# A kernel of attention and a gated feed-forward net: three passes in place of five from a maximum to a power of two and its inverse, and a new order of the whole program

## The chip, the cores and the metric

The kernel runs on one core of a Trainium2 chip. The metric is the device time of one execution in microseconds (us). The engines are TensorE (PE, matmuls), VectorE (DVE), ScalarE (ACT), GpSimd (POOL) and SyncE (SP), which only starts transfers. Each takes its instructions strictly in the order in which the program holds them, and waits by semaphores for what others produce.

## The reference

```python
def _attn_ref(q, k, v) -> np.ndarray:
    ...
    q_d = q.reshape(B, H, Sd, factor, D).mean(axis=3)
    ...
    out_d = sm_attn(q_d, k_d, v_d)
    out_up = np.repeat(out_d, factor, axis=2)
    pos = np.arange(S)
    mask = np.abs(pos[:, None] - pos[None, :]) < factor
    scores = scale * np.matmul(q, k.transpose(0, 1, 3, 2))
    scores = np.where(mask, scores, -1000000000.0)
    ...
    return (out_up + out_local).astype(np.float32)
...
def _moe_ref(x, w_in, w_spatial, b_spatial, w_out) -> np.ndarray:
    h = np.maximum(x @ w_in, 0.0)
    ...
    u, v = (h[..., :d_ff // 2], h[..., d_ff // 2:])
    ...
    v_n = (v - mu) / np.sqrt(var + 1e-06)
    v_s = np.einsum('ts,bsd->btd', w_spatial, v_n) + b_spatial[None, :, None]
    gated = u * v_s
    return (gated @ w_out).astype(np.float32)
```

q, k and v have 8 batches of 8 heads with 576 rows of 64 elements, and factor is 4; w_in is 512 x 1024, w_spatial 576 x 576, w_out 512 x 512. Attention over groups of four rows and local attention in a band of seven are added; the sum x goes through a feed-forward net with a gate along the sequence.

## The kernel before

**Numbers.** The large products are done in f16, with both factors split into a high and a low half, and three of the four partial products taken. For a factor to be split, it is first scaled by a power of two that follows from a bound on its sizes. Such a bound is made in `bound`: ScalarE sums sizes by row, TensorE turns the column of sums (L479), DVE takes the greatest (L482) and keeps its exponent (L483), TensorE spreads it over the 128 partitions into PSUM (L486), and DVE makes the power of two and its inverse from it in `exponents` (L499 to L503): a copy out of PSUM, an AND that keeps the exponent's bits, a multiply by −1 with a limit, and two passes that add constants. Eleven calls do so: the V half and the U half of w_in, w_out, and the eight batches of x. The bound of w_spatial (`columns`) takes the same function without a value from PSUM. The gate uses `bound` with passes of its own (L1105 to L1107).

**Work.** Each batch is four pieces of two heads. A piece takes sums of four rows (L720, L723), scores in the band (S, L748) with the mask either laid down by two matmuls on TensorE (L741) or added by DVE (L761), their maximum and difference (L770, L776; L764, L767 with the mask on DVE), exponentials on ScalarE (L788, L791), inverse of the row sums (L797, L801), norms (L836), the same for the down-sampled attention (Sd L810, L852 to L876), transposes (T L844, Td L891), products with v (AV L952, AVd L919), the sum xf of both (L971, L973), and the high half (xhi, L1002, ScalarE) and the low half (xlo, L1004, DVE) of x. The tiles xa to xf are x of a piece, sxa and sxb the scales of a batch, sw the scales of the weights. Then comes the net, batch by batch: V (L1029), U (L1092), the gate's product with w_spatial (SP, L1124 to L1127) with the gating on DVE (L1145, L1135), and O (L1160), twelve matmuls of 512 columns a group. The weights are decoded (L542, L547) and split into a high half on ScalarE (L510) and a low half on DVE (L513; L573 and L587 for the short last rows of w_spatial and the bias). `warm` (L1204) puts filler matmuls into TensorE's list.

**Order.** Nothing is emitted in the order of the code. Every step is an operation with an engine, a cost in ns, what it reads and writes, and a rank; `run` keeps a clock by these costs and emits for each engine the operation of least rank among those that can start within NEAR of the first. The ranks are the piece or batch number plus offsets from tables (RANK, MRANK, WRANK), less EVICT for work that empties PSUM; STAY favours the kind of matmul that TensorE is at (large f16, or the small f32 ones of the attention). Where a step can be done by one of several engines, a letter for each piece in ON says which (D DVE, P GpSimd, A ScalarE; for the mask, T TensorE and D DVE; the last letter holds for all further pieces).

```python
t, _, ask, o = min((x for x in found if x[0] <= first + near), key=lambda x: (x[1], x[0]))
...
bound(lambda: sx.ap, NP, parts, sx.sub(8), rank, powers(lambda: sx.ap, 1.0, 0.0, 30.0), 740)
...
pe_mask = sc.pick == "T"
```

Of the kernel before, what the change touches and what calls it, by code (L numbers as in the profile page):

```python
# [252 lines left out]
RANK = {"load": [143.005, 47.751, 252.982, -69.47, -172.22, -274.786, 560.411, -758.364, -311.459, 313.434, 266.06, 380.575,  # L253
            943.336, 399.915],
        "vload": [391.404, 86.345, 272.249, 337.531, 429.684, -52.69, -370.895, -252.053],
        "vabs": [509.637, -1181.093, -217.316, 87.185, -457.776, 123.004, -794.489, 144.366],
        "tv": [-183.93, 240.18, 765.617, 930.011, 56.071, -19.127, -157.242, 125.859],
        "sum": [-115.268, 142.997, -94.455, -372.167, 362.55, -75.596, 306.456, 702.576, 1696.966, 425.169, -234.075, 705.288,
            -421.357, 223.437],
        "S": [-1061.927, -157.575, 379.809, -830.223, -915.099, 670.631, 141.564, -649.896, 467.386, 88.454, 513.148, 238.256,  # L260
            245.41, 202.772],
        "E": [-534.894, -339.729, -702.236, 21.188, 160.003, 471.872, 219.972, 899.326, -409.142, -823.461, -265.585, -479.069,
            -503.017, -440.633],
        "N": [231.109, -483.572, -754.504, 524.152, -141.085, 397.308, 1325.226, -80.846, -320.013, -220.077, -64.133, -498.673,
            700.859, -253.394],
        "T": [-347.227, -440.539, -1149.413, -139.403, 917.828, -1374.545, -1166.794, 234.909, 536.972, -105.532, -561.257,
            -49.343, -383.904, -24.157],
        "Sd": [-228.884, 341.247, -989.571, 12.731, -290.563, 65.584, -210.501, 584.996, 760.783, -156.288, -493.755, 182.161,
            -206.462, -81.893],
        "Nd": [20.186, -634.328, -625.655, -47.029, -1024.698, 6.919, -369.885, -166.975, -196.395, -51.441, 745.233, 26.68,  # L270
            590.548, 680.939],
        "Td": [226.557, -226.969, 765.057, -163.935, 412.294, -360.224, 842.794, -998.859, 11.321, 28.445, -152.942, 58.045,
            -1153.807, -259.463],
        "AVd": [377.528, -777.682, -319.581, 176.718, 599.105, 1049.442, -339.489, -191.118, -286.676, -150.229, -415.778,
            -182.501, -118.84, 141.634],
        "AV": [60.151, -170.544, -717.724, 720.142, -836.725, 275.504, 440.562, -339.226, -949.724, 57.757, -184.347, -239.42,
            -4.966, -560.047],
        "X": [49.462, -601.369, 382.04, -619.469, -420.239, 803.995, 16.415, -27.426, 201.671, 266.124, -288.114, 118.52,
            -424.608, -87.751]}
MRANK = {"V": [[-120.813, 103.137], [-373.166, -785.223], [-588.287, 86.439], [-457.053, -295.554], [-271.069, 53.075],  # L280
            [-161.929, 7.172], [-384.75, 67.584], [1.753, -86.54]],
        "U0": [[-381.018, 507.475], [-225.844, -398.15], [392.079, 353.99], [415.277, -261.891], [-69.09, -16.703], [-362.251,
# [23 lines left out]
        "WO load": [201.774, -325.888, 429.457, 987.307],  # L306
        "WO decode": [137.835, 619.019, -225.889, -8.083],
        "WO bound": [-64.148, 457.463, -289.1, 18.247, -58.582],
        "WO split": [620.04, -563.746, 894.059, 1022.164]}
# [940 lines left out]
```

## Time and profile before

| | |
|---|---|
| median of three runs | 579.53 us (578.91 to 579.99) |
| profiled execution | 580.97 us, of it span 579.1 |
| PE busy | 551.6 us (95%), 6501 matmuls |
| DVE busy | 414.1 us (72%), 1084 instructions |
| ACT busy | 376.3 us (65%), 1076 instructions |
| POOL busy | 186.7 us (32%), 213 instructions |
| granted TensorE clock | 0.995 of full speed over the span |

The profile shows one execution, so its times are held against 580.97 us and not against the median. The busy shares are means over a start in which weights and the first batch are prepared (to 72.4 us), batch 0 of the net up to its first output (to 117.4 us), and the long rest, in which TensorE does the net of a batch and, between, the attention of later pieces.

### The profile page before, as it was taken

What the parts mean: (1) busy time and instruction counts of PE and PEld (TensorE: products, weight loads), DVE (VectorE), ACT (ScalarE), POOL (GpSimd) and SP (SyncE); (2) the same over time, 40 slices, a digit from 0 to 9 for tenths busy, and PEclk for the clock granted to TensorE, in tenths of its full rate; (3) what the DMA queues carried; (4) which work ended last, traced back from release to release, by engine and by line L of the source; (5) the groups of instructions that cost most, each with busy time, mean ns of one, the idle gap of its engine ahead of it and who ended that gap; (6) DMA issues with size and microseconds to landing.
All of it is one profiled execution on the core that took longest, in us unless ns stands there. A gap on an engine that the chain in (4) does not pass through costs nothing.

```text
span 579.1 us, 16048 instructions
## 1 busy us (share of the span) xinstructions
PE 551.6 (95%) x6501; PEld 368.0 (64%) x6501; DVE 414.1 (72%) x1084; ACT 376.3 (65%) x1076; POOL 186.7 (32%) x213
## 2 busy tenths in 40 slices
PE   5877899999999998999999999999999999999996
PEld 2445547764786566765776747778567567756752
DVE  5989899964898888578687776781976666844420
ACT  3689999457577677567575877565756665954422
POOL 3636533023531254154330432422422352202100
PEclk9999999999999999999999999999999999999999
DMA  8987870035322344225303343214220400010012
GB/s 285 338 241 213 215 180 1 1 102 143 88 83 91 115 103 126 65 90 138 86 20 119 99 113 102 84 65 108 77 100 2 138 2 19 8 32 1 20 54 74
DMA packets 37390, 57.04 MB, mean 99 GB/s; under 512 B 3650, under 2 KB 24130, under 8 KB 37316
## 3 DMA queue, kind: packets, MB, share of 16 engines
q1 hardware_dynamic: 35012, 48.94, 26.7%
q0 software_dynamic: 2304, 7.08, 7.2%
q8 instruction: 51, 0.84, 0.6%
q14 instruction: 23, 0.19, 0.1%
HBM read 46.57 MB, written 9.44 MB: 97 GB/s over the span
## 4 chain that ended last, share of the span: by engine, by line
PE 70%; DVE 18%; ACT 6%; issue 2%; DMA 2%; POOL 0%; SPq 0%; ACTq 0%; DVEq 0%; POOLq 0%
PE pmd L1124 4%; PE pma L1124 4%; PE pmb L1160 4%; PE pma L1160 4%; PE pmc L1029 4%; PE pmc L1160 4%; PE pma L1029 4%; PE pmc L1124 3%; PE pmb L1124 3%; PE pmd L1029 3%; PE pmd L1092 2%; PE pma L1092 2%; PE pmc L1092 2%; PE pmb L1029 2%; PE pmd L1160 2%
## 5 line engine op out<-in xcount | busy, mean ns | idle before, releaser
L1092 PEld LDWEIGHTS <-win 128*128 128x128 f16 x768 | 74.7, 98 | 20.8 <-issue 0.6
L1124 PEld LDWEIGHTS <-vha 128*128 128x128 f16 x768 | 74.0, 98 | 20.6 <-issue 2.1
L1160 PEld LDWEIGHTS <-gb 128*128 128x128 f16 x264 | 25.6, 98 | 28.5 <-issue 0.4
L1124 PE MATMUL pma<-wsp,vha 128*128 128x256 f16 (+1 forms) x216 | 29.4, 286 | 0.0
L1124 PE MATMUL pmd<-wsp,vha 128*128 128x256 f16 (+1 forms) x204 | 27.6, 285 | 1.3 <-DVE aua L1105 1.3
L1204 PE MATMUL pma<-mask_b,mask_a 128*128 128x512 bf16 x83 | 23.4, 415 | 3.1 <-DVE mask_a L383 3.1
L1124 PE MATMUL pmb<-wsp,vha 128*128 128x256 f16 (+1 forms) x180 | 24.1, 283 | 0.0
L1124 PE MATMUL pmc<-wsp,vha 128*128 128x320 f16 (+1 forms) x168 | 23.5, 290 | 0.0
L1160 PE MATMUL pmb<-wo,gb 128*128 128x512 f16 x96 | 22.0, 379 | 0.0
L1160 PEld LDWEIGHTS <-ga 128*128 128x128 f16 x120 | 11.6, 98 | 12.8 <-issue 0.2
L1057 POOL TENSOR_TENSOR sta<-sta,mhalf 128x1 f32<-128x1 f32 (+1 forms) x14 | 9.0, 646 | 32.3 <-DVE sta L1041 32.3
L669 POOL DMA_DIRECT2D tvb<-v_dram x12 | 10.8, 900 | 18.2 <-DMA tvb<-v_dram 15.7
L1160 PE MATMUL pma<-wo,gb 128*128 128x512 f16 x72 | 16.5, 379 | 0.0
L1029 PEld LDWEIGHTS <-xa 128*128 128x128 f16 x96 | 9.2, 98 | 10.8 <-issue 0.2
L1204 PEld LDWEIGHTS <-mask_a 128*128 128x128 bf16 x85 | 7.9, 104 | 12.6 <-issue 3.7
L720 POOL TENSOR_TENSOR suma<-qka 128x576 f32<-128x576 f32 x6 | 7.8, 1294 | 23.4 <-DMA qka<-qk_dram 23.4
L669 POOL DMA_DIRECT2D tva<-v_dram x12 | 10.8, 902 | 13.2 <-DMA tva<-v_dram 8.9
L1057 POOL TENSOR_TENSOR stb<-stb,mhalf 128x1 f32<-128x1 f32 (+1 forms) x15 | 10.9, 725 | 11.4 <-DVE stb L1041 11.4
L1160 PE MATMUL pmc<-wo,gb 128*128 128x512 f16 x60 | 13.8, 379 | 0.0
L1057 POOL TENSOR_TENSOR stc<-stc,mhalf 128x1 f32<-128x1 f32 (+1 forms) x11 | 7.5, 678 | 18.7 <-DVE stc L1041 15.2
L720 POOL TENSOR_TENSOR sumb<-qkb 128x576 f32<-128x576 f32 x6 | 7.8, 1296 | 16.5 <-DMA qkb<-qk_dram 16.5
L862 POOL TENSOR_SCALAR smdb<-smdb 112x3 f32<-112x3 f32 x3 | 0.6, 201 | 38.6 <-ACT eda L858 38.6
(1085 smaller groups left out, 1725.7 us busy)
## 6 DMA issues: line engine op xcount, KB each, us to landing
qka<-qk_dram SPq DMA_DIRECT2D x15, 576.0 KB, 4.9
qkb<-qk_dram SPq DMA_DIRECT2D x15, 576.0 KB, 6.2
tva<-v_dram POOLq DMA_DIRECT2D x12, 288.0 KB, 5.5
tvb<-v_dram POOLq DMA_DIRECT2D x12, 288.0 KB, 4.3
...
```

The costliest lines, as they stand in the source:

```text
L669: plan.op("POOL", 850, lambda r=r: nc.gpsimd.dma_start(t.ap[LOW:KEYS], v4[b, r], accum_op=ALU.add), w=[t], rank=rank + 2.0 + 0.3 * r, kb=2 ...
L720: side(s1).tensor_tensor(sb.ap.rearrange("p x (g r) -> p x g r", r=2), x[:, :, :, :2], x[:, :, :, 2:], op=ALU.add)
L862: side(ivd).tensor_scalar(smd.ap[:PD], smd.ap[:PD], 1.0e-9, 4.0, op0=ALU.add, op1=ALU.mult)
L1029: nc.tensor.matmul(ps.ap, xs[c].ap[:, i, t * P:(t + 1) * P], win[:, c, j, FF:], start=(c == 0 and (i, j) == (0, 0)), stop=(c == NC - 1 and ...
L1057: plan.op("POOL", 530, lambda: nc.gpsimd.tensor_tensor(st.ap[:r, 8:9], st.ap[:r, 8:9], mhalf[:r], op=ALU.pow), w=[st], rank=rank - EVICT, ...
L1092: nc.tensor.matmul(ps.ap[:, :n], win[:, c, i, ft * P:(ft + 1) * P], xs[c].ap[:, j, HA[h]:HA[h + 1]], start=(c == 0 and (i, j) == (0, 0)), ...
L1124: nc.tensor.matmul(ps.ap[:, :n], vh.ap[:, c, i, fs], wsp[:, c, j, hs], start=(c == 0 and (i, j) == (0, 0)), stop=False)
L1160: nc.tensor.matmul(ps.ap, g.ap[:, c, HA[1] * i + k:HA[1] * i + k + P], wo[:, c, j, :], start=(c == 0 and (i, j) == (0, 0)), stop=(c == NF ...
L1204: nc.tensor.matmul(ap.rearrange("p (j k) -> p j k", k=64), mask_a, mask_b[:, None, :].broadcast_to([P, 8, 64]), start=True, stop=True)
```

## The change

In `exponents` the copy out of PSUM and the AND fall away where a greatest value is given: the first pass reads PSUM itself. L483 has already cut that value to its exponent. In the bound of w_spatial all four passes stay. The cost that the planner holds for the step goes from 740 to 480 ns. Besides, all tables of ranks, EVICT, NEAR, STAY and the choices of engines are other numbers; of them the diff shows a line or two.

```diff
-RANK = {"load": [143.005, 47.751, 252.982, -69.47, -172.22, -274.786, 560.411, -758.364, -311.459, 313.434, 266.06, 380.575,
...
+RANK = {"load": [172.616, 163.506, 233.678, -41.931, -272.276, -420.051, 403.181, -910.109, -387.176, 364.033, 578.994, 368.324,
...
-EVICT = 456.633
+EVICT = 631.446
...
-NEAR = 104.496
-STAY = 26.882
+NEAR = 100.31
+STAY = 38.419
...
-        "mask": "TTTTTTTTD",
+        "mask": "TTTTTTTTDDDTTDDDDDDDDDDDDTD",
...
 
     def exponents(t, most, up, fac, low):
         e, sc, iv = (t().bitcast(I32)[:, i:i + 1] for i in (7, 8, 9))
-        if most is not None:
-            nc.vector.tensor_copy(t()[:, 7:8], most)
-        nc.vector.tensor_scalar(e, e, 0x7F800000, None, op0=ALU.bitwise_and)
-        nc.vector.tensor_scalar(e, e, -1.0, -low * 2.0**23, op0=ALU.mult, op1=ALU.min)
+        if most is None:
+            nc.vector.tensor_scalar(e, e, 0x7F800000, None, op0=ALU.bitwise_and)
+            most = e
+        else:
+            most = most.bitcast(I32)
+        nc.vector.tensor_scalar(e, most, -1.0, -low * 2.0**23, op0=ALU.mult, op1=ALU.min)
         nc.vector.tensor_scalar_add(sc, e, (268.0 - up) * 2**23)
         nc.vector.tensor_scalar(iv, e, -1.0, (up - 14.0 + fac) * 2**23, op0=ALU.mult, op1=ALU.add)
 
@@ -648,7 +650,7 @@
                 plan.op("ACT", 130 + act(n), lambda i=i, c=c, t=t, n=n: nc.scalar.activation(junk[:, :n], t.ap[:, :n], AF.Abs, accum_out=sw[:, i, c:c + 1]),
                         r=[t], w=[("sum", k, c)], rank=rank, name="wabs")
                 toks.append(("sum", k, c))
-            bound(lambda i=i: sw[:, i], len(toks), toks, ("sw", i), WRANK[k + " bound"][-1], powers(lambda i=i: sw[:, i], 0.0, 16.0 if k == "WO" else 0.0, 30.0), 740)
+            bound(lambda i=i: sw[:, i], len(toks), toks, ("sw", i), WRANK[k + " bound"][-1], powers(lambda i=i: sw[:, i], 0.0, 16.0 if k == "WO" else 0.0, 30.0), 480)
         for done, t, n in later[k]:
             wtok[k] += done()
 
@@ -690,7 +692,7 @@
         sx, iv = sx_of[b]
         rank = NP * b + 1.0 + RANK["vabs"][b]
         parts = [sx.sub(p) for p in range(NP)]
-        bound(lambda: sx.ap, NP, parts, sx.sub(8), rank, powers(lambda: sx.ap, 1.0, 0.0, 30.0), 740)
+        bound(lambda: sx.ap, NP, parts, sx.sub(8), rank, powers(lambda: sx.ap, 1.0, 0.0, 30.0), 480)
 
         for i in range(2):
             plan.op("DVE", 120, lambda i=i: nc.vector.tensor_scalar(iv.ap[:, i:i + 1], sw[:, i, 9:10], sx.ap[:, 9:10], None, op0=ALU.mult),
```

The mask now lies on TensorE for pieces 0 to 7, 11, 12 and 25, before for 0 to 7 alone. Behind `exponents`, whose three passes are now L503 to L505, the new file's lines are two higher (L1004 is L1006, L513 is L515).

DVE's list at the scale of batch 0 (tile sxa). Before, five passes, then the maxima of the down-sampled attention, then the low halves xb and xa of batch 0:

```order
L499 COPY sxa<-pmb 128x1
L500 TENSOR_SCALAR sxa<-sxa 128x1
L501 TENSOR_SCALAR sxa<-sxa 128x1
L502 TENSOR_SCALAR sxa<-sxa 128x1
L503 TENSOR_SCALAR sxa<-sxa 128x1
L852 TENSOR_REDUCE mxdc<-pab 112x2
L853 TENSOR_REDUCE mxdc<-pmd 112x1
L854 TENSOR_SCALAR mxdc<-mxdc 112x3
L780 TENSOR_SCALAR mxc<-mxc 128x10
L696 TENSOR_SCALAR sx2a<-sw,sxa 128x1
L1004 SCALAR_TENSOR_TENSOR xb<-xfb,sxa,xb 128x576
L1004 SCALAR_TENSOR_TENSOR xa<-xfa,sxa,xa 128x576
```

Now, with decoding of weights (L549) between:

```order
L503 TENSOR_SCALAR sxa<-pmc 128x1
L504 TENSOR_SCALAR sxa<-sxa 128x1
L505 TENSOR_SCALAR sxa<-sxa 128x1
L549 SCALAR_TENSOR_TENSOR mbb<-more,mbb 128x512
L698 TENSOR_SCALAR sx2a<-sw,sxa 128x1
L549 SCALAR_TENSOR_TENSOR mbd<-more,mbd 128x512
L1006 SCALAR_TENSOR_TENSOR xb<-xfb,sxa,xb 128x576
L1006 SCALAR_TENSOR_TENSOR xa<-xfa,sxa,xa 128x576
```

The two passes are gone, and the low halves follow behind other work than before.

DVE's list at the low splits of w_spatial (wsp, wsp_lb) beside batch 0's fourth low half (xd). Before:

```order
L1004 SCALAR_TENSOR_TENSOR xd<-xfa,sxa,xd 128x576
L573 SCALAR_TENSOR_TENSOR wsp_lb<-wstc,sw,wsp_hh 64x576
L587 SCALAR_TENSOR_TENSOR wsp_lb<-bh,sel,biasa 2x576
L589 MEMSET vt_100 2x512
L852 TENSOR_REDUCE mxdd<-paa 112x2
L853 TENSOR_REDUCE mxdd<-pmc 112x1
L854 TENSOR_SCALAR mxdd<-mxdd 112x3
L513 SCALAR_TENSOR_TENSOR wsp<-wsta,sw,wsp 128x576
L513 SCALAR_TENSOR_TENSOR wsp<-wstb,sw,wsp 128x576
```

Now, some 25 rows ahead of the first low half of batch 0, with the maxima and differences of a later piece (L772, L778) between:

```order
L589 SCALAR_TENSOR_TENSOR wsp_lb<-bh,sel,biasa 2x576
L591 MEMSET vt_100 2x512
L515 SCALAR_TENSOR_TENSOR wsp<-wsta,sw,wsp 128x576
L772 TENSOR_REDUCE mxc<-paa 128x10
L778 TENSOR_TENSOR sa<-paa,mxc 128x2x3x64
L778 TENSOR_TENSOR sa<-paa,mxc 128x2x2x64
L515 SCALAR_TENSOR_TENSOR wsp<-wstb,sw,wsp 128x576
L515 SCALAR_TENSOR_TENSOR wsp<-wstc,sw,wsp 128x576
```

Before, the splits follow xd; now they stand ahead of xa to xd.

TensorE's list where the scores of piece 11 (qkb, kdc) begin. Before:

```order
L919 MATMUL pab<-pdTa,tva 64x144 x8
L952 MATMUL pab<-probTb,vc 64x60 x2
L952 MATMUL pab<-probTb,vc 64x58 x2
L952 MATMUL pab<-probTb,vc 64x56 x2
L952 MATMUL pab<-probTb,vc 64x58 x10
L952 MATMUL pab<-probTb,vc 64x54 x2
L952 MATMUL pab<-probTb,vc 64x58 x2
L748 MATMUL paa<-qkb 64x64 x20
L810 MATMUL paa<-kdc 64x144 x4
L810 MATMUL pmc<-kdc 64x144 x2
```

Now:

```order
L893 MATMUL pma<-perm,edb 100x112 x3
L893 MATMUL pmd<-perm,edb 100x112 x3
L846 MATMUL pab<-ident,sa 128x128 x5
L743 LDWEIGHTS mask_a
L743 MATMUL paa<-mask_b,mask_a 128x320
L743 LDWEIGHTS mask_a
L743 MATMUL paa<-mask_b,mask_a 128x320
L750 MATMUL paa<-qkb 64x64 x20
L812 MATMUL paa<-kdc 64x144 x4
L812 MATMUL pmb<-kdc 64x144 x2
```

Two mask matmuls of 320 columns stand ahead of the scores (L748, now L750), and the piece comes behind other work than before.

## Rows read from the trace of the kernel before

**Rows 1.** Busy time of each engine by stretch (windows), from the first O matmul of batch 0 to 300 us and from there to the end of the last matmul. Columns: stretch and its length in us, then for each engine busy us (instructions), the granted clock of TensorE (PEclk), the DMA share and GB/s.

```profile
117.36:300.00 182.64, 179.94 (x2284) 122.28 (x2282) 139.19 (x354) 124.47 (x368) 70.12 (x72) 1.00 0.36 99
300.00:574.10 274.10, 274.06 (x2998) 183.97 (x2996) 171.26 (x457) 161.66 (x471) 69.40 (x77) 1.00 0.22 63
```

**Rows 2.** Timeline of TensorE at the end. Columns: start us, us, engine, line, operation, tile written <- tiles read, shape, count; in brackets the idle time of the engine before it and what ended that.

```profile
571.36 2.75 PE L1175 MATMUL pmd<-wo,gta 128*128 128x512 f16 x12
```

**Rows 3.** Busy time of each engine by stretch ahead of the first O matmul; the columns are those of rows 1.

```profile
14.00:36.00 22.00, 17.66 (x198) 9.28 (x194) 18.73 (x41) 13.86 (x43) 12.39 (x15) 0.94 0.95 286
36.00:50.00 14.00, 11.10 (x214) 7.29 (x214) 13.43 (x40) 13.96 (x40) 5.42 (x7) 1.00 0.96 292
50.00:72.40 22.40, 18.05 (x371) 11.92 (x369) 20.65 (x54) 21.46 (x62) 13.71 (x14) 1.00 0.76 197
72.40:100.00 27.60, 27.23 (x189) 16.83 (x188) 26.62 (x70) 26.04 (x65) 9.77 (x11) 1.00 0.39 95
100.00:117.36 17.36, 16.02 (x164) 12.67 (x163) 16.31 (x53) 9.55 (x23) 1.26 (x1) 1.00 0.00 1
```

**Rows 4.** Timeline of TensorE: the first V group of batch 0, the one long wait in its gating, the first O group. Columns as in rows 2.

```profile
72.42 0.82 PE L1029 MATMUL pmb<-win,xa 128*128 128x512 f16 x3
...
106.17 1.11 PE L1124 MATMUL pmd<-wsp,vha 128*128 128x320 f16 x7 [1.34 <-DVE aua L1105]
...
117.36 2.75 PE L1160 MATMUL pmb<-wo,gb 128*128 128x512 f16 x12
```

**Rows 5.** Timeline of VectorE: the first three passes of the exponents of w_in's V half (L499 to L501), and the read of a size bound out of PSUM in the gating of batch 0 (L1105).

```profile
38.73 0.16 DVE L499 COPY sw<-pmc 128x1 f32<-128x1 f32 x1
38.92 0.15 DVE L500 TENSOR_SCALAR sw<-sw 128x1 int32<-128x1 int32 x1
39.11 0.15 DVE L501 TENSOR_SCALAR sw<-sw 128x1 int32<-128x1 int32 x1
...
105.98 0.14 DVE L1105 TENSOR_SCALAR aua<-pmd 128x1 f32<-128x1 f32 x1
```

**Rows 6.** Timeline of VectorE: one row for each kind of work whose place differs between the two orders: sums of four rows (L720, L723), inverse of the row sums (L797, L801), norm of the local weights (L836), sums of the two attentions (L971, L973), norm of the down-sampled weights (L876), the low half of batch 0's fourth piece (L1004), a low split of w_spatial (L573), a memset (L589).

```profile
9.67 0.75 DVE L720 TENSOR_TENSOR suma<-qka 128x576 f32<-128x576 f32 x1
...
10.46 0.46 DVE L723 TENSOR_TENSOR kda<-suma 128x288 f32<-128x288 f32 x1
...
22.28 0.17 DVE L797 TENSOR_SCALAR smb<-smb 128x10 f32<-128x10 f32 x1
...
22.48 0.22 DVE L801 RECIPROCAL smb<-smb 128x10 f32<-128x10 f32 x1
...
24.06 0.81 DVE L836 TENSOR_TENSOR sb<-sb,smb 128x640 f32<-128x640 f32 x1
...
46.70 0.69 DVE L971 TENSOR_TENSOR xfa<-pab,dna 128x232 f32<-128x232 f32 x2
...
47.31 0.26 DVE L973 TENSOR_TENSOR xfa<-pab,dna 128x112 f32<-128x112 f32 x1
...
57.39 0.93 DVE L876 TENSOR_TENSOR edb<-edb,smda 112x432 f32<-112x432 f32 x1
...
71.54 0.81 DVE L1004 SCALAR_TENSOR_TENSOR xd<-xfa,sxa,xd 128x576 f16<-128x576 f32 x1
72.26 0.81 DVE L573 SCALAR_TENSOR_TENSOR wsp_lb<-wstc,sw,wsp_hh 64x576 f16<-64x576 f32 x1
...
73.95 0.48 DVE L589 MEMSET vt<- 2x512 f16 x1
```

**Rows 7.** Timeline of VectorE: four rows that last longer than others of their line and shape, and behind the last of them the next row of its line and shape.

```profile
25.63 1.02 DVE L797 TENSOR_SCALAR sma<-sma 128x10 f32<-128x10 f32 x1
...
26.81 2.40 DVE L720 TENSOR_TENSOR suma<-qka 128x576 f32<-128x576 f32 x1
...
44.88 1.17 DVE L854 TENSOR_SCALAR mxda<-mxda 112x3 f32<-112x3 f32 x1
...
50.36 1.48 DVE L542 TENSOR_SCALAR mba<-rowa 128x512 int32<-128x512 int32 x1
51.77 0.41 DVE L542 TENSOR_SCALAR mbc<-rowc 128x512 int32<-128x512 int32 x1
```

**Rows 8.** Timeline of GpSimd at two of these times.

```profile
27.45 1.14 POOL L720 TENSOR_TENSOR sumb<-qkb 128x576 f32<-128x576 f32 x1
...
49.77 1.79 POOL L836 TENSOR_TENSOR sb<-sb,smb 128x640 f32<-128x640 f32 x1 [0.51 <-DVE smb L801]
```

**Rows 9.** The chain of work that ended last, two O groups that follow each other. Columns: start us, us, engine, tile, line, count.

```profile
306.57 2.70 PE pmc L1160 x12
309.27 2.59 PE pmd L1160 x12
```

**Rows 10.** Timeline of TensorE: a mask pair and the scores behind it, and the three longest waits behind the first O.

```profile
40.30 0.43 PE L741 MATMUL pab<-mask_b,mask_a 128*128 128x320 bf16 x2
...
40.66 0.81 PE L748 MATMUL pab<-qka 64*64 64x64 f32 x40
...
225.88 0.76 PE L844 MATMUL pab<-ident,sc 128*128 128x128 f32 x5 [0.71 <-DVE sc L836]
...
230.66 0.27 PE L479 MATMUL pma<-ident,sxa 128*4 128x128 f32 x1 [0.76 <-ACT junk L686]
...
266.10 0.73 PE L844 MATMUL pab<-ident,sc 128*128 128x128 f32 x5 [0.81 <-DVE xfb L973]
```

More of the change, by code (lines that the diff above doesn't have):

```diff
@@ L247, in run @@
         return end
-RANK = {"load": [143.005, 47.751, 252.982, -69.47, -172.22, -274.786, 560.411, -758.364, -311.459, 313.434, 266.06, 380.575,
[L254 to L279, printed above, removed]
@@ L294 @@
-EVICT = 456.633
-WRANK = {"WV load": [31.22, -21.921, 242.309, 4.474],
-        "WV decode": [350.543, -287.444, -567.367, 661.466],
-        "WV bound": [-83.736, 162.235, 909.503, 36.755, -835.361],
-        "WV split": [-201.598, 11.031, -341.826, -1007.43],
-        "WU load": [-364.293, 427.826, 390.089, -59.831],
-        "WU decode": [387.574, -316.232, 1019.795, 459.568],
-        "WU bound": [1425.684, -228.293, 245.85, 118.051, 725.352],
-        "WU split": [-187.848, -607.313, -258.771, -328.661],
-        "WSP load": [289.708, -579.107, 622.627, -316.354, 744.76],
-        "WSP bound": [397.382, 106.669, -930.598, 200.751, 873.332, -382.338],
-        "WSP split": [-150.625, -91.686, 309.424, 430.824, -1165.74],
[L306 to L309, printed above, removed]
@@ new lines @@
+EVICT = 631.446
+WRANK = {"WV load": [-41.769, 18.139, 189.494, 58.805],
+        "WV decode": [458.518, -401.667, -479.197, 770.702],
+        "WV bound": [-163.371, 252.141, 901.76, 252.185, -1085.175],
+        "WV split": [-127.832, -29.375, -339.014, -1111.487],
+        "WU load": [-228.164, 502.441, 368.068, -132.82],
+        "WU decode": [360.434, -336.811, 995.885, 403.396],
+        "WU bound": [1591.637, -218.673, 8.433, 7.413, 721.344],
+        "WU split": [-209.57, -786.56, -188.078, -276.18],
+        "WSP load": [251.363, -480.883, 635.016, -193.234, 849.963],
+        "WSP bound": [-68.866, -28.646, -819.709, 284.273, 924.284, -319.903],
+        "WSP split": [-335.437, -282.535, 326.202, 214.697, -1170.617],
+        "WO load": [147.025, -435.719, 405.236, 997.492],
+        "WO decode": [243.416, 628.263, -94.556, -9.624],
+        "WO bound": [-149.166, 511.753, -275.329, 116.145, 62.382],
+        "WO split": [728.738, -569.268, 908.419, 1143.808]}
@@ L320 @@
 UPN = 0
-ON = {"sub": "DDDDDDADDADAAADDDADDAAADDDA",
-        "inv": "DDDDDPDDPDDPDPPDPDPDDPDPDDDPPPPD",
-        "invd": "DDDPDPPDDPDDDDDDPPDDPPDDDDPPPPD",
-        "sum": "DPPPDPPPDDPDPPDDDDPPDPDDDDPDDDPD",
-        "mask": "TTTTTTTTD",
-        "norm": "PDPPPDPDPPDDDPDPPPDPDPDPPPPDDPD",
-        "normd": "PAAPPDPPAAADDPAAPAPADAAPPPPADDAP",
-        "vlo": "PDPDPPPDDPDPDPDDDDPDDPPDDDPDPDDPDPDPDPD"}
+ON = {"sub": "DADDDDDAADDADAADDDDDAADDADADDA",
+        "inv": "DDDDDDPDDPPDDDPPDDPDPPDPDPPPPPD",
+        "invd": "DDDPPDPDDDDDPDDPDDPPDDDDPPPPPPD",
+        "sum": "DPPPPPDDDDDPDPPPDPPDDPDPPPPDPPD",
+        "mask": "TTTTTTTTDDDTTDDDDDDDDDDDDTD",
+        "norm": "DDPPPDDPDDDDDDPPDPPDPDPDPPDDPDDP",
+        "normd": "PAAPPPAPAPPADADAPPAADAPAPPDDDPDA",
+        "vlo": "DDPPPDDPPPDPPDDDPPDDDPDDDPDPDDPPPPDPPPD"}
 @with_exitstack
```

54 lines of the change are left out of this document (40 added, 14 removed).

## The prediction

> **What bounds the kernel now.** I read three views in turn: engine time by stretch, TensorE's timeline at the borders of those stretches, and VectorE's rows inside them. From the first batch's first O matmul on, TensorE is the bound: from 117.36 to 300 us it works 179.94 of 182.64 us, and from 300 to the last matmul 274.06 of 274.10 [rows 1]. The rest of the run is fixed to that: the last O group starts at 571.36 [rows 2], and its eviction and output transfer end the span at 579.1. So the time is the moment of the first O, plus TensorE's work behind it, plus its 2.7 us of waits (182.64 − 179.94), plus a tail that both orders share.
>
> The moment of the first O is not set by TensorE. Between 14 and 72.40 us TensorE works 46.81 of 58.40 us, VectorE (DVE) 52.81, ScalarE 49.28 [rows 3]. The reader should see that DVE is the fullest (90%), and that it runs at 96% from 36 to 50 us and again from 72.4 to 100. The first V matmul, at 72.42, waits for batch 0 of x, whose four low halves DVE writes; the last, xd's, starts at 71.54 and takes 0.81 [rows 6]. From there to 117.36 are 44.94 us in which TensorE waits 1.71: 0.37 up to 100 us [rows 3], and 1.34 in one wait at 106.17, for an `aua` that DVE reads out of PSUM at 105.98 [rows 4, 5].
>
> **The change, part by part.** (1) *The passes.* At 38.73 the copy starts, and the third pass, the multiply, 0.38 us behind it [rows 5]. Two passes fewer give that 0.38 in each of 11 calls: 4.2 us of DVE. Nine of the calls lie behind the first V or, WU's, just beside it; where DVE has 171.26 busy of 274.10 us and TensorE 99.99% [rows 1], they cover nothing, so I book zero there. Two (WV's and batch 0's) lie ahead of the first V for certain. Would a first pass that reads PSUM be dearer? A TENSOR_SCALAR from PSUM takes 0.138 us in the row at 105.98, the old third pass from SBUF 0.15, the copy from PSUM 0.16 [rows 5]: no surcharge, I book none; the bounds are ±0.01 us a pass by these rows.
>
> [...]
>
> (2) *DVE ahead of the first V.* The order moves far more than the passes save. Before batch 0's fourth low half, DVE now has four more low splits of w_spatial and the two short-row ones (six at 0.81, as L573's and xd's), the memset (0.48), one pair of sums (0.75 + 0.46), one row-sum inverse (0.17 + 0.22), two norms (0.81 each) and the three passes of WU's bound (0.15 each): 4.86 + 0.48 + 1.21 + 0.39 + 1.62 + 0.45 = 9.01 us. Gone from there are two copies and two ANDs (0.60), one `edb` norm (0.93) and one pair of xf sums (0.69 + 0.26): 2.48. Net +6.5 us [rows 5, 6]. DVE is in order, so behind the moved splits stand the scale of WU, the sums of xf and the four xlo that the first V needs.
>
> What can hide 6.5 us? First, DVE's idle time from 14 to 72.4: 58.40 − 52.81 = 5.6 us [rows 3]. Second, slowed instructions: four rows are far longer than their likes, L720 2.40 against 0.75, L542 1.48 against 0.41, L797 1.02 against 0.17, L854 1.17 against the same 0.17: 1.65 + 1.07 + 0.85 + 1.00 = 4.6 us, two of them beside a GpSimd instruction on SBUF [rows 6 to 8]. Bounds: nothing recovered gives +6.5; all of both recovered gives 6.5 − 5.6 − 4.6 = −3.7. For the middle I take a rate that DVE does hold: 13.43 of 14.00 us from 36 to 50 [rows 3]. 52.81 + 6.5 = 59.3 us at 0.959 take 61.8 us in place of 58.4, +3.4; if one of the four slowed rows (1.15 each on the mean) does not come back, **+2.3**. ScalarE has 9.1 us idle in the same stretch [rows 3], TensorE 11.6; the ten fillers that TensorE gets more are 512 columns as O's are, 2.59 / 12 = 0.22 us each [rows 9], and lie in that idle time. I book both at nothing; without the cover the fillers cost 2.2.
>
> (3) *From the first V to the first O.* The work that came ahead is missing here: DVE has at least 6.5 us less between the two moments, where it was 96% busy up to 100 us [rows 3]. The 1.34 us wait ended when DVE had done the read of PSUM [rows 4, 5]; with a shorter queue in front it should shrink. Bounds nothing and −1.7 (all of TensorE's idle time in the stretch); I take **−1.0**, three quarters of the one wait. The first O then comes at 117.36 + 2.3 − 1.0 = 118.7.
>
> (4) *TensorE behind the first O.* Three more masks are done on TensorE: a mask pair starts 0.36 us before the scores behind it, so 1.08 us [rows 10]. The order interleaves small f32 matmuls with the large f16 ones in 33 stretches in place of 30; a group of twelve at such a border takes 2.70 against 2.59 us [rows 9]; with two borders that is 0.22 each, 0.6 in all (half of that if only one border pays). **+1.7**; nothing hides it, since TensorE is the bound.
>
> (5) *TensorE's waits behind the first O.* 2.7 us now, of it 0.71 at 225.88 and 0.81 at 266.10, both for DVE, and 0.76 at 230.66 for a size sum of ScalarE [rows 10]. The masks that leave DVE belong to pieces 11, 12 and 25, and pieces 11 and 12 are prepared around there. I take the waits down to 0.7, **−2.0**; bounds: nothing, and −2.7.
>
> The sum is 2.3 − 1.0 + 1.7 − 2.0 = **+1.0 us**. It is made against the profiled execution, 580.97 us (span 579.1 and 1.9 around it), which lies 1.44 over the median of the runs, 579.53. So: 582.0 in a profile, 580.5 as a median. 0.2% (1.16 us) is about what a measurement of this kernel can tell from no change; +1.0 is 0.17%, inside it.
>
> **The rivals.** *The order packs better (faster).* DVE's idle time is taken whole and half of the slowed rows' excess less a little (1.9) goes: 6.5 − 5.6 − 1.9 = −1.0 at the first V; the wait of 1.34 goes: −1.5 with what else is idle there; all 2.7 of the later waits go against 1.7 of work: −1.0. Together −3.5: 576.0. For it: the moved work lies early, where DVE has holes (18.73 of 22.00 us from 14 to 36 [rows 3]). Against: those holes are waits for loads and for TensorE, which queued work need not fit.
>
> *The added work lands in full (slower).* Place: DVE's queue ahead of batch 0's first xlo, where the four w_spatial splits now stand. If they run at a time when x would have been ready, none of the 6.5 hides: +6.5 − 1.0 + 1.7 − 1.3 = +5.9, that is 585.4. It decides from a first V beyond 75.8, the upper end of the likeliest case (+3.4, no slowed row gone). Against it: 5.6 us of idle DVE.
>
> *The masks are not repaid (slower).* TensorE's 1.7 us come for certain, the waits stay: they were for DVE's norm and xf sums and for ScalarE, not for a mask by name [rows 10]. +1.3 + 1.7 = +3.0: 582.5.
>
> *More collisions of DVE and GpSimd (slower).* L720 at 26.81 ran beside GpSimd's sum from 27.45, and L542 at 50.36 beside its norm from 49.77 [rows 7, 8]. In the new order the splits meet GpSimd's sums and norms elsewhere; with three more such collisions at about 1.3 (mean of 1.65 and 1.07) the first V is 3.9 later than in the likeliest case: +1.0 + 3.9 = +4.9, 584.4. [...]
>
> **How the numbers follow.** The likeliest case 0.44; better packing 0.34; full landing 0.10; masks not repaid 0.07; collisions 0.05. The likeliest is 580.5, and its own range is 579.4 (first V at +1.2, two slowed rows gone) to 581.6 (first V at +3.4); what of it lies above 580.7, a first V later than +2.5, is already slower, and I give that part 0.08. So faster 0.34, same 0.36, slower 0.08 + 0.10 + 0.07 + 0.05 = 0.30. The range of 8 in 10 goes from 575.0, between the faster rival's 576.0 and its bound with every slowed row gone (579.5 − 3.7 − 1.5 − 1.0 = 573.3), to 584.2, which leaves out the full landing, half of the collisions and, I think, a fifth of the faster side: 0.10 + 0.02 + 0.07.
>
> **What the profile after would show.** Right: no copy from PSUM ahead of the exponents, and first passes from PSUM of 0.14 to 0.16 us; first V at 74 to 75.5, first O at 118 to 119.5; 22 mask matmuls; waits of TensorE behind the first O under 1 us; between the first O and the last matmul some 456.4 us (456.74 + 1.7 − 2.0). Wrong: a first V at 79 (landing in full), or at 71 (packing); TensorE waits of 2 us and more for DVE behind 117 us; rows of DVE above 1.2 us that a row of GpSimd covers, in greater number than four. The part I trust least is the first V: one number out of an order that I can count, but whose waits I can't read.

## The result, and the profile after

The changed kernel takes 583.99 us (median; 583.52 to 584.25), the kernel before on the same chip 579.70: a ratio of 1.0075 (95% interval 1.0058 to 1.0093), 4.3 us slower. The profiled execution took 583.84 us with a span of 582.0. The profiles differ by 2.9 us only, because the profiled execution of before lies 1.3 us above that median and the one of after 0.15 below.

Three stretches of the profile after, columns as in [rows 1]: from 72.4 us, from 100 us to the first O, and from the first O to the end of the last matmul. They answer to [rows 1, 3].

```profile
72.40:100.00 27.60, 27.60 (x272) 17.81 (x270) 24.21 (x70) 26.85 (x72) 8.49 (x10) 1.00 0.27 70
100.00:118.11 18.11, 18.11 (x181) 14.29 (x180) 13.39 (x39) 8.87 (x28) 1.50 (x2) 1.00 0.00 1
118.11:577.10 458.99, 455.17 (x5286) 307.55 (x5283) 309.24 (x785) 278.51 (x805) 154.66 (x163) 1.00 0.27 77
```

TensorE's timeline after: batch 0's bound is turned (L479), the first V, the first O. They answer to [rows 2, 4].

```profile
64.26 0.27 PE L479 MATMUL pmc<-ident,sxa 128*4 128x128 f32 x1 [3.60 <-ACT junk L688]
...
75.42 0.82 PE L1031 MATMUL pma<-win,xa 128*128 128x512 f16 x3
...
118.11 2.75 PE L1162 MATMUL pmc<-wo,gb 128*128 128x512 f16 x12
```

The same turn of batch 0's bound in the kernel before:

```profile
58.23 0.27 PE L479 MATMUL pmb<-ident,sxa 128*4 128x128 f32 x1 [0.81 <-ACT junk L686]
```

The longest waits of TensorE behind the first O after, summed by what they were for (us in total, times, longest); they answer to [rows 10].

```profile
PE pma L486 <- DVE aue L483: 1.1, 1, 1.1
PE pma L486 <- DVE aub L483: 0.6, 1, 0.6
PE pmc L486 <- DVE sxb L483: 0.5, 1, 0.5
PE paa L750 <- ACT probTa L848: 0.5, 1, 0.5
```

What to read here. The first V comes at 75.42 in place of 72.42 (+3.0). From there to the first O are 42.69 us in place of 44.94, with no wait left (TensorE works 27.60 of 27.60 and 18.11 of 18.11): −2.25. Behind the first O the program takes 458.99 us in place of 456.74: 455.17 of work in place of 454.00 (+1.2), and 3.8 of waits in place of 2.7 (+1.1). 3.0 − 2.25 + 2.25 = +3.0; the span says 2.9, the tail is the same 5 us. The three long waits of before [rows 10] are all gone; three new ones are for DVE's L483, the last step of a size bound ahead of its spread, and the rest for ScalarE's and DVE's attention steps.

What stands ahead of L483 at the longest of them can be read. TensorE turns the sums of `aue` at 372.69, and DVE, which is to take their greatest (L482), first does two steps of the maxima of later attention work (L856, L772) and reaches L482 at 374.18:

```profile
372.69 0.27 PE L479 MATMUL pma<-ident,aue 128*1 128x128 f32 x1
...
372.66 0.87 DVE L856 TENSOR_SCALAR mxdb<-mxdb 112x3 f32<-112x3 f32 x1
373.45 0.81 DVE L772 TENSOR_REDUCE mxb<-pab 128x10 f32<-128x640 f32 x1
```

No run varies this place alone.

### The profile page after: what moved, and what is told of

It reads as the page before. It is cut to its first block, busy times and chain, and to the rows that moved or that the text cites. A ratio compares the mean times of both kernels' runs of the same rounds, so it can differ in the third digit from the quotient of the medians.

```text
span 582.0 us, 16063 instructions
## 1 busy us (share of the span) xinstructions
PE 555.9 (96%) x6517; PEld 371.0 (64%) x6517; DVE 409.5 (70%) x1047; ACT 371.5 (64%) x1055; POOL 197.6 (34%) x224
## 4 chain that ended last, share of the span: by engine, by line
PE 70%; DVE 12%; ACT 9%; DMA 2%; POOL 2%; issue 2%; SPq 1%; ACTq 0%; POOLq 0%; DVEq 0%
PE pmb L1031 4%; PE pmb L1126 4%; PE pmc L1126 4%; PE pma L1126 4%; PE pmc L1094 4%; PE pmc L1162 4%; PE pmd L1162 4%; PE pma L1031 4%; PE pmd L1094 4%; PE pma L1094 3%; PE pmb L1094 3%; PE pma L1162 3%; PE pmd L1031 3%; PE pmd L1126 3%; DMA wsta<-wT_dram 2%; PE pmc L1031 2%
## 5 line engine op out<-in xcount | busy, mean ns | idle before, releaser
L722 POOL TENSOR_TENSOR sumb<-qkb 128x576 f32<-128x576 f32 x10 | 12.2, 1225 | 64.6 <-DMA qkb<-qk_dram 64.6
L1126 PE MATMUL pmb<-wsp,vha 128*128 128x256 f16 (+1 forms) x216 | 29.1, 284 | 0.0
L1126 PE MATMUL pma<-wsp,vha 128*128 128x320 f16 (+1 forms) x192 | 26.5, 287 | 0.0
L1126 PE MATMUL pmc<-wsp,vha 128*128 128x256 f16 (+1 forms) x192 | 26.2, 286 | 0.0
L1126 PE MATMUL pmd<-wsp,vha 128*128 128x256 f16 (+1 forms) x168 | 22.9, 286 | 0.4 <-ACT edb L860 0.4
L1162 PE MATMUL pma<-wo,gb 128*128 128x512 f16 x84 | 19.3, 379 | 0.0
L1059 POOL TENSOR_TENSOR sta<-sta,mhalf 128x1 f32<-128x1 f32 (+1 forms) x15 | 10.9, 727 | 23.5 <-DVE sta L1043 23.5
L1162 PE MATMUL pmc<-wo,gb 128*128 128x512 f16 x72 | 16.5, 379 | 0.0
L1162 PE MATMUL pmd<-wo,gb 128*128 128x512 f16 x72 | 16.5, 379 | 0.0
L1162 PE MATMUL pmc<-wo,ga 128*128 128x512 f16 x48 | 11.0, 379 | 0.0
```

Of the source, the lines that this page charges most:

```text
L722: side(s1).tensor_tensor(sb.ap.rearrange("p x (g r) -> p x g r", r=2), x[:, :, :, :2], x[:, :, :, 2:], op=ALU.add)
L1059: plan.op("POOL", 530, lambda: nc.gpsimd.tensor_tensor(st.ap[:r, 8:9], st.ap[:r, 8:9], mhalf[:r], op=ALU.pow), w=[st], rank=rank - EVICT, ...
L1126: nc.tensor.matmul(ps.ap[:, :n], vh.ap[:, c, i, fs], wsp[:, c, j, hs], start=(c == 0 and (i, j) == (0, 0)), stop=False)
L1162: nc.tensor.matmul(ps.ap, g.ap[:, c, HA[1] * i + k:HA[1] * i + k + P], wo[:, c, j, :], start=(c == 0 and (i, j) == (0, 0)), stop=(c == NF ...
```

## The experiments

**The passes alone.** Tables and planner cost of before, the code of the three passes; all engines keep their order.

```diff
-            nc.vector.tensor_copy(t()[:, 7:8], most)
-        nc.vector.tensor_scalar(e, e, 0x7F800000, None, op0=ALU.bitwise_and)
-        nc.vector.tensor_scalar(e, e, -1.0, -low * 2.0**23, op0=ALU.mult, op1=ALU.min)
...
+            most = most.bitcast(I32)
+        nc.vector.tensor_scalar(e, most, -1.0, -low * 2.0**23, op0=ALU.mult, op1=ALU.min)
```

> The kernel before with its own tables and its own planner cost of 740, and only the three passes in place of five: every engine keeps its order, DVE loses 22 instructions. Theory A (the passes are hidden, the new order makes the difference): within 0.2% of before, 579.0 to 580.5 us, first V at 72.0 to 72.5, first O 117.0 to 117.4. Theory B (4.2 us of DVE are worth something, since DVE is the fullest engine ahead of the first V): faster by 0.4 to 1.5 us, first V at 71.7 or earlier.

Measured: 578.71 us against 579.47, ratio 0.9982 (0.9972 to 0.9993). The first V, the wait near 105, and the stretch from the first O (at 116.27) on:

```profile
71.99 0.82 PE L1031 MATMUL pmb<-win,xa 128*128 128x512 f16 x3
...
105.08 1.11 PE L1126 MATMUL pmd<-wsp,vha 128*128 128x320 f16 x7 [1.03 <-DVE aua L1107]
...
116.27:572.61 456.34, 453.65 (x5280) 306.33 (x5277) 308.75 (x801) 285.45 (x838) 139.02 (x149) 1.00 0.28 78
```

The first V is 0.43 us earlier, the first O 1.09 (the wait for `aua` is 1.03 in place of 1.34), and behind it are 456.34 us in place of 456.74. By the time theory B holds, by a small sum: the median is 0.8 us lower (0.4 to 1.6 by the interval), below the 579.0 us that theory A allowed. The first V does not decide, 71.99 where B wanted 71.7 or earlier and A 72.0 to 72.5. This is also the fastest version of the study, faster than both kernels.

**The order alone.** The new tables and the cost of 480, with the five passes put back.

```diff
-        if most is None:
-            nc.vector.tensor_scalar(e, e, 0x7F800000, None, op0=ALU.bitwise_and)
...
+        if most is not None:
+            nc.vector.tensor_copy(t()[:, 7:8], most)
+        nc.vector.tensor_scalar(e, e, 0x7F800000, None, op0=ALU.bitwise_and)
```

> The kernel after with the five passes put back and the cost of 480 kept: the new order alone, DVE has 22 instructions more. Theory A (the order makes the difference): as after, 583.5 to 584.7 us, that is 0.7 to 0.9% above before. Theory B (the passes are worth something): 0.4 to 2 us slower than after, 584.5 to 586.

Measured: 584.28 us, ratio to before 1.0087 (1.0070 to 1.0103). The first V, and the stretch from the first O on:

```profile
76.20 0.82 PE L1029 MATMUL pma<-win,xa 128*128 128x512 f16 x3
...
119.03:578.46 459.43, 455.54 (x5286) 307.50 (x5283) 311.15 (x795) 278.47 (x805) 154.63 (x163) 1.00 0.28 77
```

The loss is the new order's: +0.87% with the five passes of before, and theory A holds. What the passes cost in this order is not resolved: the medians differ by 0.3 us with intervals that overlap, and the first V by 0.8 (76.20 against 75.42), which is about what two profiles of one list differ by (see the run on the masks). Against the order of before with three passes, the kernel after is 5.3 us slower (583.99 − 578.71); on profiles 1.84 us of it lie at the first O (118.11 − 116.27) and 2.65 behind (458.99 − 456.34).

**What makes the first V late: fillers and clock?** In the profile after TensorE stands idle for 3.60 us ahead of batch 0's bound, and the eight fillers behind it run at a granted clock of 0.66. One run leaves the eight out, one fills the idle time with 15 more.

```diff
-        for _ in range(count):
+        for _ in range(0 if count == 8 else count):
```

> The kernel after without the eight filler matmuls that stand between the spread of batch 0's bound and the products with v; they took 3.09 us at 65.52 in the profile after, at a granted clock of 0.66. Theory C (fillers at half clock push back xf, xc, xd and so the first V): first V at 73.5 to 74.3 in place of 75.42, all later times follow, 582.3 to 583.0 us. Theory D (DVE's queue sets the first V): first V stays at 75 or later and the time within 0.1% of after.

```diff
-        for _ in range(count):
+        for _ in range(38 if count == 23 else count):
```

> The kernel after with 15 more fillers in the group at 55.7 us, so that the 3.60 us in which TensorE stood idle ahead of batch 0's bound are filled and the granted clock should stay at 1.00. Theory C (the fall of the clock to 0.66 between 65 and 70 us costs about 1.3 us in the eight fillers and 0.6 in the products behind them): first V at 73.6 to 74.2, 582.2 to 583.0 us. Theory D (DVE's queue sets the first V): clock 1.00, first V at 75 or later, time as after within 0.1%.

Measured: 586.61 us without the eight (ratio 1.0126, 1.0110 to 1.0142), 583.88 with 15 more (1.0077, 1.0063 to 1.0091). Windows without the eight, in which the third figure from the end is the granted clock:

```profile
65.00:70.00 5.00, 3.27 (x83) 2.74 (x82) 4.93 (x14) 4.26 (x12) 0.18 (x1) 0.50 0.96 252
70.00:75.00 5.00, 4.50 (x33) 3.36 (x32) 3.29 (x14) 3.53 (x8) 3.06 (x3) 0.51 0.73 144
```

TensorE's products with v (L954) and the first V there:

```profile
67.00 1.54 PE L954 MATMUL paa<-probTb,vd 64*64 64x58 f32 x38
...
77.11 0.82 PE L1031 MATMUL pma<-win,xa 128*128 128x512 f16 x3
```

The window from 60 to 75 us with 15 more fillers:

```profile
60.00:75.00 15.00, 12.60 (x216) 7.48 (x217) 13.98 (x38) 13.82 (x35) 4.41 (x5) 1.00 0.81 184
```

TensorE there: the eight fillers, the products with v, the wait for xf, the first V:

```profile
65.62 1.90 PE L1206 MATMUL pma<-mask_b,mask_a 128*128 128x512 bf16 x8
...
70.83 0.72 PE L921 MATMUL pab<-pdTa,tvb 64*64 64x144 f32 x16 [0.81 <-DVE xfb L975]
...
75.39 0.82 PE L1031 MATMUL pma<-win,xa 128*128 128x512 f16 x3
```

Theory C falls on both sides. With the clock at 1.00 throughout, the eight fillers take 1.90 us in place of 3.09 and the products with v end 1.5 us earlier (69.06 against 70.57), but then TensorE waits 0.81 for DVE's xf, and the first V is at 75.39. Without the eight the clock is granted at 0.50 to 0.51 from 65 to 75 us, the product of 38 matmuls takes 1.54 us in place of 0.87, and the first V is 1.7 later. The fillers earn their place; they are not what is late. Theory D's forecast that nothing changes came true with 15 more and failed without the eight; whether it has the right queue is the next question.

**DVE's queue or ScalarE's?** In the profile after ScalarE (ACT) does w_spatial's high splits ahead of batch 0's last two size sums (L688 on vc and vd). Timeline of ScalarE: the first and the last of w_spatial's high halves, then the sums:

```profile
53.88 0.78 ACT L574 ACTIVATE wsp_hh<-wstc,sw 128x576 f16<-128x576 f32 x1
...
59.55 0.78 ACT L512 ACTIVATE wsp<-wstb,sw 128x576 f16<-128x576 f32 x1
...
61.76 0.73 ACT L688 ACTIVATE junk<-vc 128x640 bf16<-128x640 f32 x1
...
63.37 0.74 ACT L688 ACTIVATE junk<-vd 128x640 bf16<-128x640 f32 x1
```

One run moves only DVE's low splits of w_spatial (with the memset) behind batch 0's xlo, the next ScalarE's splits as well. Both keep all other lists; the names `wls` and `whs` mark the splits of w_spatial.

```diff
-            if emit:
-                o.fn()
+            if emit and o.name in ('wls', 'lb') and done < 4:
+                kept.append(o.fn)
+            elif emit: o.fn()
+            if o.name == "xlo": done += 1; done == 4 and [f() for f in kept]
```

> The kernel after with one thing moved in VectorE's list alone: the four low splits of w_spatial, the two short-row ones and the memset (5.3 us) stand behind batch 0's fourth low half in place of ahead of its scale; all other lists are as after. Theory D (DVE's queue sets the first V): first V 2.5 to 3.5 us earlier, at 72 to 73. Theory E (ScalarE's queue sets it: the high splits of w_spatial and the bias stand ahead of the size sums of batch 0, and its bound comes at 64.26 in place of about 58): batch 0's bound stays at 64.0 to 64.3, first V at 74.3 or later, gain at most 1.1 us. First O: at most as much earlier, and later if the splits now stand in the way of the gating.

```diff
-            if emit and o.name in ('wls', 'lb') and done < 4:
+            if emit and o.name in ('wls', 'lb', 'whs', 'hh', 'bh') and done < 4:
```

> As the run before, and on ScalarE too the four high splits of w_spatial, that of the short rows and the two passes on the bias (5.3 us) stand behind batch 0's fourth high half. TensorE and GpSimd as after. Theory E: batch 0's bound at 59 to 60 in place of 64.26, first V at 71.5 to 72.5. Theory D: no earlier than in the run before. Theory F (work ahead of the first V is only swapped with work behind it): first O within 0.7 us of after's 118.1 all the same, time 583.3 to 584.7 us; else first O near 115.5 and 581 to 582 us.

Measured: 588.64 us with DVE's splits moved (1.0146, 1.0121 to 1.0171), 587.22 with both (1.0129, 1.0110 to 1.0147). TensorE with DVE's splits moved: batch 0's bound, and the longest wait behind the first V, which is at 75.79:

```profile
64.43 0.37 PE L481 MATMUL pmc<-ident,sxa 128*4 128x128 f32 x1 [3.60 <-ACT junk L690]
...
84.20 0.16 PE L488 MATMUL pmb<-sxb,ones_b 4*128 4x1 bf16 x1 [2.95 <-DVE sxb L485]
```

DVE there, the first step of that bound on DVE:

```profile
64.84 0.28 DVE L484 TENSOR_REDUCE sxa<-pmc 4x1 f32<-4x128 f32 x1 [4.62 <-PE pmc L481]
```

TensorE with both moved, where the first V is at 72.27: batch 0's bound, and the longest wait:

```profile
61.60 0.27 PE L481 MATMUL pmc<-ident,sxa 128*4 128x128 f32 x1 [1.52 <-ACT junk L690]
...
79.74 0.37 PE L481 MATMUL pmb<-ident,sxb 128*4 128x128 f32 x1 [4.71 <-ACT junk L690]
```

ScalarE there, its two waits ahead of batch 0's last size sums, and the last moved high split:

```profile
55.08 0.38 ACT L862 ACTIVATE eda<-pab,mxdc 112x144 f32<-112x144 f32 x1 [1.66 <-PE paa L752]
...
57.56 1.03 ACT L877 ACTIVATE eda<-eda,smdc 112x144 f32<-112x144 f32 x3 [0.99 <-POOL smdc L868]
...
75.88 0.76 ACT L514 ACTIVATE wsp<-wstb,sw 128x576 f16<-128x576 f32 x1
```

From the first V to the first O, in the kernel after, with DVE's splits moved, and with both moved; then 5 us behind the long wait with both moved (the third figure from the end is the granted clock):

```profile
75.42:118.11 42.69, 42.69 (x360) 29.58 (x357) 35.44 (x102) 32.70 (x90) 9.30 (x10) 1.00 0.14 40
...
75.79:124.38 48.59, 45.64 (x361) 31.26 (x358) 39.93 (x109) 32.86 (x90) 9.29 (x10) 0.93 0.15 37
...
72.27:122.27 50.00, 45.29 (x361) 30.06 (x357) 40.85 (x110) 37.69 (x98) 9.29 (x10) 0.93 0.16 39
...
80.00:85.00 5.00, 5.00 (x14) 1.56 (x12) 4.88 (x11) 2.90 (x7) 0.67 (x1) 0.53 0.10 23
```

Theory D falls: with 5.3 us less in DVE's list the bound stays at 64.43 and the first V at 75.79, and DVE stands idle for 4.62 us until TensorE has turned the bound. Theory E holds in its kind: with ScalarE's splits out of the way too, the bound comes at 61.60 and the first V at 72.27, 3.15 earlier than after's. The bound was to come at 59 to 60; ScalarE now waits 1.66 us for TensorE and 0.99 for GpSimd ahead of the sums, so about half of the 5.3 us comes through. ScalarE's splits were not moved alone, because DVE's low splits read the high ones.

Of theory F the kind holds and the size doesn't: the first O was to stay within 0.7 us of after's, and comes 4.2 us later (6.3 where only DVE's moved). The moved splits now stand ahead of batch 1's bound, and TensorE waits 4.71 us for its size sum (2.95 for DVE's step where only DVE's moved). The wait is not all of it: behind it the clock is granted at 0.53 over 5 us (0.50 from 85 to 90 us where only DVE's moved), and TensorE is busy 2.6 us longer (2.95) than after for the same work. The gap and the slower clock behind it together are the 7.3 us (5.9) by which this stretch grew.

**The splits behind batch 1's bound too.** The same edit, released behind the fifth scale in place of the fourth xlo.

```diff
-            if emit and o.name in ('wls', 'lb', 'whs', 'hh', 'bh') and done < 4:
+            if emit and o.name in ('wls', 'lb', 'whs', 'hh', 'bh') and done < 5:
...
-            if o.name == "xlo": done += 1; done == 4 and [f() for f in kept]
+            if o.name == "scale": done += 1; done == 5 and [f() for f in kept]
```

> The kernel after with all of w_spatial's splits (ScalarE's and VectorE's, as in the run that moved both) put behind the bound of batch 1 in place of ahead of batch 0's. Theory E with F (the splits delay whatever bound stands behind them in ScalarE's list; with none behind them, the gain at the first V stays): first V at 71.8 to 72.8, from the first V to the first O 42.7 to 44.5 us with no single wait over 1.5, first O at 115 to 117, 581 to 583 us. Rival (VectorE and ScalarE are full between the first V and the first O, so the 5.3 us push the gating back wherever they stand): first O at 118 or later, 584 us or more.

Measured: 588.63 us (1.0145, 1.0127 to 1.0163). TensorE: the longest wait behind the first V; then the stretch from the first V to the first O:

```profile
95.18 0.37 PE L481 MATMUL pmd<-ident,sw 128*4 128x128 f32 x1 [4.93 <-ACT junk L652]
...
73.15:123.41 50.26, 45.33 (x361) 31.07 (x358) 40.55 (x109) 37.55 (x97) 9.31 (x10) 0.93 0.17 38
```

The rival's times hold, its reason less so. The first V keeps most of its gain (73.15), but now w_out's bound is late: 4.93 us for a size sum of ScalarE. Behind this wait too the clock is granted at 0.50 (95 to 100 us), TensorE is busy 2.6 us longer, and the first O comes at 123.41. VectorE and ScalarE were not full in the stretch (40.55 and 37.55 of 50.26 us). In both runs that moved ScalarE's 5.3 us, the bound that follows them in its list is late by nearly as much.

**The three masks.** The mask matmuls of pieces 11, 12 and 25 are left out.

```diff
-            if pe_mask:
+            if pe_mask and n < 2 * NP:
```

> The kernel after with the mask matmuls of pieces 11, 12 and 25 left out (six matmuls; these pieces' scores stay unmasked), all else in its order. Theory G (behind the first O every TensorE matmul adds its time): 1.1 us faster than after, 582.5 to 583.2, TensorE busy behind the first O 1.1 less, waits within 0.3 of after's 3.8. Theory H (the waits are for DVE and ScalarE and take up what TensorE saves): the time within 0.3 us of after, the waits 0.8 to 1.1 more.

Measured: 584.13 us, ratio 1.0073 (1.0058 to 1.0088), against 1.0075 for after. The stretch from the first O to the end, and the waits there that grew:

```profile
118.80:577.90 459.10, 454.45 (x5280) 306.92 (x5277) 309.13 (x785) 278.50 (x805) 154.42 (x163) 1.00 0.28 77
```

```profile
PE paa L750 <- ACT probTa L848: 0.8, 1, 0.8
...
PE pab L846 <- DVE xfb L975: 0.6, 1, 0.6
```

The time agrees with theory H: it is that of after, and not 1.1 us less. TensorE's work falls by 0.7 us (454.45 against 455.17), and its waits grow from 3.8 to 4.6: that for `probTa` from 0.5 to 0.8, that for xf from 0.2 to 0.6, and one for GpSimd's norm is new with 0.4. The stretch is 459.10 us against 458.99. That the saved work went into these waits is likely but not shown: in the five other traces whose order behind the first O is after's (without the eight, with 15 more, and the three with moved splits), the waits there are 2.8 to 4.4 us and the work 454.8 to 455.4. The first V of this profile is 76.11 against 75.42, though nothing ahead of it differs: one profile pins the first V to no better than 0.7 us.

**Bounds first.** The passes alone in the order of before, and in DVE's list every step that a bound needs moved ahead of up to two others.

```diff
+            if o.eng == "DVE" and o.name not in ('great', 'scale', 'most'):
+                if late:
+                    flush()
+                kept.append(o)
+                while len(kept) > 2:
+                    kept.pop(0).fn()
...
             if emit:
-                o.fn()
+                give(o)
```

> The kernel with the three passes in the order of before, and in VectorE's list alone each instruction group that a bound needs (greatest, scale, the maximum ahead of it) moved ahead of up to two others that stood before it and that it doesn't depend on. Theory K (TensorE's wait of 1.2 to 1.3 us near 106 is only the place of the read of PSUM in VectorE's list): that wait falls under 0.6, first O 0.5 to 1.0 us earlier than 116.27, the rest within 0.3 us, 577.7 to 578.4 us. Rival (what is pushed back, low halves and norms, is waited for in turn): no faster than 578.7, with waits of TensorE for xf, x or norms of 0.5 us and more.

Measured: 581.23 us, ratio to before 1.0027 (1.0015 to 1.0039), that is 2.5 us slower than the passes alone. Waits of TensorE between the first V and the first O, and the first O (lines are 21 higher here):

```profile
104.80 1.79 PE L1147 MATMUL pmd<-wsp,vha 128*128 128x320 f16 x12 [0.25 <-DVE aua L1128]
...
107.23 1.79 PE L1147 MATMUL pmc<-wsp,vha 128*128 128x320 f16 x12 [0.37 <-DVE uf L1168]
...
115.50 1.47 PE L1147 MATMUL pmd<-wsp,vha 128*128 128x256 f16 x12 [0.36 <-DVE ub L1168]
...
117.03 2.75 PE L1183 MATMUL pmb<-wo,gb 128*128 128x512 f16 x12
```

Theory K is right on the one wait (0.25 in place of 1.03) and wrong on the time: what was pushed back, the gating of uf and ub, is waited for with 0.37 and 0.36 us, and the first O is at 117.03 in place of 116.27. That is 0.8 of the 2.5 us; in the profile another 1.1 come behind the first O, where the waits are 3.3 us in place of 2.7. The rival's time holds, though the waits that are new up to the first O are for the gating and under its 0.5 us.

**The old tables with the new cost.** All tables of before, cost 480 at both places, three passes.

```diff
-        bound(lambda: sx.ap, NP, parts, sx.sub(8), rank, powers(lambda: sx.ap, 1.0, 0.0, 30.0), 740)
+        bound(lambda: sx.ap, NP, parts, sx.sub(8), rank, powers(lambda: sx.ap, 1.0, 0.0, 30.0), 480)
```

> The kernel with three passes, the planner's cost of 480 and all tables of before: nothing was searched anew, but the planner makes an order of its own from the new cost. Theory I (a table is worth something only with the costs it was searched for; any other cost gives an order of no merit): 0.5 to 2.5% slower than before, 582 to 594 us. Theory J (tables carry over, the lower cost only moves a few instructions): within 0.3% of before, 578 to 581 us.

Measured: 628.90 us, ratio 1.0848 (1.0828 to 1.0869). The longest wait of TensorE:

```profile
PE pmc L479 <- ACT junk L688: 15.4, 1, 15.4
```

Theory I holds, and the loss is far above what I expected of it: 260 ns less in the cost of a step that stands in the program eleven times gave an order that is 49 us slower, 15.4 of it one wait for a size sum of ScalarE. In this case the tables hold only for the cost that they were used with; one other cost was tried.

## Why the prediction came out as it did

The likeliest case, no measurable change, did not come. The time is slower, by 4.3 us where +1.0 was the sum, and 584.0 lies inside the range by 0.2 us only. Of the signs that were named, the first passes (0.139 to 0.158 us from PSUM), the first V, the first O and the 22 mask matmuls came as said; waits under 1 us behind the first O, and 456.4 us from there, did not. Step by step:

(1) *The passes.* I booked 0.6 us ahead of the first V, and nothing for the nine other calls, where TensorE was to cover them. The passes alone gave 0.43 at the first V, 0.66 between first V and first O (half of it the wait for `aua`) and 0.4 behind, 0.8 in the medians: a term of the right order. The three parts are differences of two profiles, whose first V alone can differ by 0.7 us; the medians carry the sum. The first pass from PSUM cost nothing extra here. Groups of line L503 after, two of those from PSUM, with the shortest and the longest of the eleven calls, and then the one from SBUF (ns, least, median, greatest):

```profile
L503 DVE TENSOR_SCALAR sxa<-pmc x2: 139/145/151, 66.0 to 235.1; 128x1 int32<-128x1 int32 x2
...
L503 DVE TENSOR_SCALAR sxa<-pma x1: 158/158/158, 355.5 to 355.5; 128x1 int32<-128x1 int32 x1
...
L503 DVE TENSOR_SCALAR sw<-sw x1: 153/153/153, 53.3 to 53.3; 128x1 int32<-128x1 int32 x1
```

From PSUM a pass takes 139 to 158 ns, the one from SBUF 153, inside that spread.

(2) *Ahead of the first V.* +3.0 was measured where I had +2.3, about one profile's scatter apart, but the step failed in its cause, and the near number is luck. I summed DVE's queue, took it to run at its fullest rate (96%), and booked ScalarE at nothing, since it had 9.1 us of idle time. It was ScalarE's list that held the first V: its splits of w_spatial and the bias stand ahead of batch 0's size sums, so the bound is turned at 64.26 in place of 58.23. Moving DVE's 5.3 us away did nothing; moving ScalarE's too brought 3.15. Idle time over the whole stretch says nothing of a chain that runs through one engine's list at one place. DVE did not fill up either: in the kernel after it works 56.11 of the 61.42 us from 14 us to the first V, 91%, and is idle 5.3 us where before it was 5.6.

```profile
14.00:75.42 61.42, 48.42 (x764) 29.49 (x763) 56.11 (x141) 54.33 (x152) 27.82 (x31) 0.94 0.92 255
```

(3) *First V to first O.* Right in sign, too small: −2.25 where I had −1.0. The bound of −1.7 was passed: all waits there went, 1.7 us and not three quarters of one, and TensorE had half a microsecond less to do there, which the bound left out. DVE's share fell from 96% to 88% up to 100 us (24.21 of 27.60).

(4) *Work behind the first O.* +1.2 against +1.7. The six mask matmuls were booked at 1.08; without them TensorE works 0.7 us less. That leaves 0.1 to 0.5 for the three more borders of f32 and f16 stretches, which single profiles do not resolve. The 0.6 booked for them let both borders of a stretch pay, but the group of 2.59 us [rows 9] itself ends at a border (TensorE goes over to f32 at 311.69), so by these rows only the first one pays, 0.3. "Nothing hides it" isn't borne out: without the masks the time stayed the same.

(5) *Waits behind the first O.* This step came out with the other sign, and it is the largest error of the sum. I took them from 2.7 to 0.7, since the masks leave DVE where its waits stood. Those waits did go, but other ones came: +1.1 in place of −2.0, an error of 3.1 us in a sum that is off by 2.0 on profiles. (The five other traces of this order have +0.1 to +1.7.) I had counted what an order takes away at places that I knew, and nothing for places where it makes new waits. The rival on masks that are not repaid, with a chance of 0.07, has the nearest sum, +3.0 by +1.3 at the first O and +1.7 behind it, where +0.75 and +2.25 came; but it let the old waits stay, and they went, so that its number too is in part luck.

Of the other rivals, the full landing did not happen: it needed +6.5 at the first V, and +3.0 came. Its sign, a first V beyond 75.8, was too near to tell, since another profile of the same list has 76.11. Better packing did not come either: the first V was later and not earlier, and what was won between it and the first O is work that had moved ahead. More collisions did not come: ahead of the first V after has three DVE rows that last more than 0.5 us longer than their likes (at 25.17, 38.33 and 41.24 us), before had four [rows 7].

The sum stood on the profiled execution of before, which is 1.3 us above its median. On medians the change is +4.3, on profiles +2.9; what lies between is one execution's scatter. Left open: why the search took this order, which of its tables makes the waits for L483 behind the first O, and what of the 2.25 us there each of them and the masks is worth; no run takes these waits away.
